# Scaling the values of four blocks in two halves, and one of these scalings at another place in GpSimd's queue

## The chip, the cores and the metric

The kernel runs on one core of one Trainium2 chip. The metric is the device time of one execution in microseconds (us), shorter is better; the time given for a kernel is the median of several runs. Before the change it was 153.32 us, median of 3 runs (153.32 to 153.71).

A core has five engines that run their own instruction queues in order and wait for each other through semaphores: TensorE (PE, matrix products; its weight loads are listed apart as PEld), VectorE (DVE), ScalarE (ACT), GpSimd (POOL) and SyncE (SP, which only issues transfers here). Transfers between device memory and the core's working memory are carried by 16 DMA engines, whichever queue issued them.

## What is computed

Two layers, one behind the other, on 4 sequences of 768 tokens. The first is a recurrence with 8 heads of width 64, each with its own decay; the second a feed-forward layer of the RWKV kind on its output.

```python
gamma = 1 - 2 ** (-5 - arange(H)); scale = 1 / sqrt(D)
for t in range(S):                                   # per batch b and head h
    state = gamma * state + outer(k[t], v[t])        # 64 x 64
    y[t] = scale * (q[t] @ state)
x = y with heads side by side                        # 4 x 768 x 512
xk = mu_k * x + (1 - mu_k) * x_prev                  # x_prev: one token before
xr = mu_r * x + (1 - mu_r) * x_prev
out = sigmoid(xr @ w_r) * (relu(xk @ w_k) ** 2 @ w_v)
```

Inputs and output are float32; matrix products take float16 operands.

## The kernel before

**Blocks.** The tokens are cut into 12 blocks of 256 (block n is tokens 256·(n mod 3) of sequence n div 3), and the recurrence is done block by block in its parallel form. For a block, with keys K, queries Q and values V: V is multiplied by a power of the head's decay, a different one for each token (`VS`, float16); K and Q are turned by PE; PE makes scores from them, DVE masks these (`A2`); PE makes the output from the masked scores and `VS`, and from Q and the state that the blocks before left; PE makes the block's share of the state from K and `VS`. Then comes the feed-forward layer of the block.

**Three kinds of blocks.** A block has 256 tokens and the memory 128 partitions, so two tokens lie in each partition, as i = 0 and 1. In blocks 0 and 1 these are neighbours (tokens 2p and 2p + 1). In blocks 2 to 5 (`WIDE`) and 6 to 11 (`HALF`) they are tokens p and p + 128: i = 0 is the first half of the block, i = 1 the second, and each half comes with a transfer of its own (256 KB of values each). In memory, `V32(n)` holds for each partition 8 heads x 128 numbers, i = 0 and 1 side by side within a head; `VS(n)` holds all of i = 0 ahead of all of i = 1. There are 4 buffers `V32` and 3 buffers `VS`, taken in turn.

**The order is written out by hand.** `ORDER` is a list of words, one for each step, such as `vs.3~p`: code `vs` (scale the values), block 3, engine p (p POOL, v DVE, a ACT, s SP); a number after @ names the banks of PE's result memory. The loop at the end of the kernel reads the words from the first to the last and emits each step's instructions, so that each engine's queue has its steps in the order of the list. Waits follow from what a step reads and writes. The steps that matter here:

- `lq`, `lk`, `lv`: load queries, keys, values of a block (function `load`); nearly all are issued by POOL. In a load of a block from 2 on, `lk` and `lv` are two transfers each. One transfer costs POOL an instruction (L230 or L235 in the profile).
- `vs`: scale the values (`scale_v`, L253). It is one instruction on DVE for ten of the blocks and on POOL for blocks 1 and 3.
- `C`: the block's share of the state, on PE (`state`; L384 for blocks 2 to 5). Blocks 2 and 5 are the last of their sequences; there the loop takes i = 0 alone. For blocks 3 and 4 it takes i = 0 and i = 1. `C` reads `VS`.
- `U`: the state carried on (`summed`; L419 on DVE, L241 for `U.3.0`, a copy on ACT). `G`: the state decayed (`decayed`, L424 on ACT).
- `S`, `M`: scores (L331) and their mask (L354, DVE). `I`, `Y`: output from the state (L441) and from the scores (L478), which reads `VS` too. `D`: output to the feed-forward layer's input (L514, DVE). `Tq`, `Tk`: queries and keys turned (L272, L278).
- `K`, `Qa`, `Qb`: product with w_k (L582 and L572), ReLU (L591), square (L603). `R`, `s`: product with w_r (L612), sigmoid (L618). `V`, `O`: product with w_v (L624), final product (L630). `wv`: load of w_v (L742).

The stretch of the list that the change touches, and what follows it up to the next loads:

```
lq.5~p Ek.3~a K.2.2@5 Qa.2.2~a K.2.3@4 M.4.1~v M.4.0~v Qa.2.3~a Qb.2.3~a lk.6~p S.3.1@67 M.3.1~v
S.3.0@01 vs.3~p C.3@23 U.3.0~a Qb.2.2~a K.2.1@4 Qa.2.1~a K.2.0@2 Qa.2.0~a I.3@45 lq.6~p vs.4~v
C.4@67 U.3.1~v X.2.1.1~v V.0.1.0@3 M.3.0~v V.1.0.0@2 G.3~a U.4.0~v I.4@01 X.2.1.3~v U.4.1~v J.3
Qb.1.3~a Y.4 Qb.2.0~a lk.5~p X.2.1.2~v ...
```

So POOL's queue is there: lq.5, lk.6 (two transfers), vs.3, lq.6, lk.5 (two), lk.7 (two), lv.5 (two). In the built program each load that POOL issues also waits, where its turn comes, for the landing of the load that POOL issued eight places before it: the loads take eight semaphores in turn. So lk.6's second transfer waits for the first half of lv.3, and what lk.6's first one waits for landed before that. C.3 writes banks 2 and 3, which S.4.0 had before, so that it waits for M.4.0 on DVE as well as for vs.3.

Of the kernel before, what the change touches and what calls it, by code (L numbers as in the profile page):

```python
# [30 lines left out]
X.0.0.1~v t.0.1.2~a X.0.0.2~v Tk.2@0 t.0.1.3~a t.0.0.0~a M.1.0~v X.0.0.0~v z.2@4 Y.1 t.0.1.1~a
X.0.0.3~v Ek.2~a K.0.0@0 K.0.1@6 lq.4~p U.1.1~v G.1~a wr~p lk.4~p D.1~v dx.1~v X.1.0.2~v X.1.0.0~v
K.0.2@1 Qa.0.0~a Qb.0.0~a Qa.0.2~a lq.3~p X.1.0.1~v X.1.0.3~v X.1.1.0~v Qa.0.1~a K.0.3@0 Qa.0.3~a
lk.3~p vs.2~v Tq.2@1 X.1.1.2~v K.1.3@6 K.1.0@0 C.2@7 U.2.0~v lv.3~p Eq.2~a S.2.1@23 M.2.1~v S.2.0@45
M.2.0~v Qb.0.3~a lv.4~p K.1.1@1 X.1.1.1~v Qa.1.0~a t.0.1.0~a K.1.2@7 I.2@23 Qb.0.1~a Qa.1.1~a wv.0~p
Qb.0.2~a Tq.4@01 Eq.4~a Y.2 Qa.1.3~a Qb.1.1~a X.0.1.3~v X.1.1.3~v R.1.1@4 Tk.4@01 Ek.4~a J.2 R.1.0@6
# [6 lines left out]
J.4 D.4~v dx.4~v R.2.0@6 Qb.2.1~a V.0.0.1 O.0.0~v X.3.0.1~v Eq.5~a Qb.1.2~a V.1.0.1 X.3.0.2~v
O.1.0~v Tq.6@01 Eq.6~a Tk.6@45 Ek.6~a st.0.0~s lk.7~p st.1.0~s V.1.1.0@3 V.1.1.1 O.1.1~v s.2.0~a
R.2.1@0 s.2.1~a lv.5~p X.3.0.0~v X.3.0.3~v Tk.7@67 Ek.7~a G.4~a S.6@45 M.6~v Tk.5@23 Ek.5~a vs.5~v
V.2.0.0@0 K.3.2@1 Qa.3.2~a K.3.0@6 S.5.0@23 M.5.0~v S.5.1@45 C.5@1 U.5.0~v K.3.3@7 Qb.3.2~a Qa.3.0~a
lq.7~p K.3.7@6 Qa.3.3~a Qa.3.7~a lv.6~p lq.8~p vs.6~v M.5.1~v V.2.0.1 st.0.1~s I.5@67 O.2.0~v
st.2.0~s C.6@23 U.6.0~a U.6.1~v U.6.2~v K.3.6@1 Qa.3.6~a lk.9~p X.3.1.3~v Y.5 Tq.7@45 Eq.7~a U.6.3~v
X.3.1.2~v I.6@01 J.5 X.3.1.0~v D.5~v X.3.1.1~v Qb.3.3~a G.6~a V.2.1.0@2 K.3.1@3 V.2.1.1 O.2.1~v
Qb.3.7~a Qa.3.1~a Qb.3.1~a dx.5~v K.3.4@4 K.3.5@5 Qa.3.5~a X.5.0.0~v X.5.0.3~v R.3.1@2 s.3.1~a  # L50
lv.7~p Qa.3.4~a X.5.0.1~v Qb.3.4~a R.3.0@5 R.4.0@2 s.3.0~a s.4.0~a Qb.3.0~a X.5.0.2~v vs.7~v K.5.2@4
S.7@67 st.1.1~s M.7~v Qb.3.5~a Y.6 Qb.3.6~a lv.10~p C.7@23 U.7.0~v X.5.1.1~v Qa.5.2~a K.5.0@5
R.4.1@6 Qa.5.0~a D.6~v s.4.1~a V.4.0.0@4 V.4.0.1 V.3.1.0@5 U.7.1~v Qb.5.0~a X.5.1.3~v U.7.2~v I.7@01
X.5.1.2~v U.7.3~v Tq.8@67 Eq.8~a X.5.1.0~v O.4.0~v lv.8~p vs.8~v Qb.5.2~a lq.10~p lk.8~p Tk.8@23
# [30 lines left out]
def kernel(  # L85
# [136 lines left out]
    def load(x, d, split, a=None):
        def go(e, n, j0=0, j1=NJ):
            b, t0 = n // NB, n % NB * TM
            hs = slice(2 * j0, 2 * j1)
            src = x[b, hs, t0 : t0 + TM, :]
            dst = staged(a)[:, hs] if (a, n, j0) in EARLY else d(n)[:, hs]
            if split and (half(n) or wide(n)):
                for i in range(2):
                    e.dma_start(  # L230
                        out=dst[:, :, i * D : i * D + D],
                        in_=src[:, i * P : i * P + P].rearrange("h p d -> p h d"),
                    )
            else:
                e.dma_start(out=dst, in_=src.rearrange("h (p i) d -> p h (i d)", i=2))  # L235

        return go
# [12 lines left out]
        return go  # L250

    def scale_v(e, n):
        e.tensor_tensor(  # L253
            out=VS(n), in0=V32(n).rearrange("p h (i d) -> p i h d", i=2),
            in1=gks[:, int(half(n) or wide(n)), :, :, None].to_broadcast([P, 2, H, D]), op=ALU.mult,
        )
# [543 lines left out]
```

## Time and profile before

| what | us |
|---|---|
| time, median of 3 runs | 153.32 (153.32 to 153.71) |
| time of the profiled execution | 153.28 |
| its span, first to last instruction | 151.4 |
| PE busy | 143.4 (95%) |
| DVE busy | 127.8 (84%) |
| ACT busy | 103.6 (68%) |
| POOL busy | 55.3 (37%), all of it in the first 76 us |

The granted clock of PE was 1.000 over the whole span. The profile consists of a page (busy time, the span in 40 slices, the chain of work that ended last, the costliest groups of instructions) and of views asked from the trace. A row of a timeline gives the start, the duration of a run of equal instructions from the start of its first to the end of its last, the engine, the line, the operation, what it writes and reads, the shape, the count, and in brackets how long the engine was idle before it and what ended this. Instructions on one engine may overlap slightly in such rows, since the next one starts before the last one's end.

### The profile page before, as it was taken

Reading aid. Unit: us, or ns where it says so; the run is one execution under the profiler, and the core shown is the slowest. Engines: PE = TensorE matmul, PEld = TensorE weight load, DVE = VectorE, ACT = ScalarE, POOL = GpSimd, SP = SyncE. Lnnn points to the kernel's source line nnn. Section 1 sums busy time; section 2 is a strip of 40 time slices with the busy share of each in tenths; the row PEclk is TensorE's granted clock in tenths of the full one; section 3 lists DMA queues with packets and bytes.
Section 4 is the critical chain, followed back from the end, with each engine's and each line's share of the span. In section 5 each row is a group of like instructions: output and inputs, shape, how many; then the busy total and the mean of one; then the engine's idle time right before and its main releaser. Section 6 shows DMA issues by size and latency. Waiting matters only on the chain.

```text
span 151.4 us, 5541 instructions
## 1 busy us (share of the span) xinstructions
PE 143.4 (95%) x2426; PEld 82.8 (55%) x2426; DVE 127.8 (84%) x212; ACT 103.6 (68%) x195; POOL 55.3 (37%) x65
## 2 busy tenths in 40 slices
PE   7878799999999999999999999999999999999991
PEld 3345487757754554547465564548456444655450
DVE  7886999999989999999999999999799999400432
ACT  3565979899844795779567786999604756839420
POOL 7953998577957309996710000000000000000000
PEclk9999999999999999999999999999999999999999
DMA  5999999999999999999999019301000005500433
GB/s 140 219 229 197 207 231 192 168 251 212 196 167 202 233 262 107 256 300 198 231 173 126 7 38 283 105 35 45 0 4 0 4 0 211 205 0 0 148 133 139
DMA packets 45624, 22.16 MB, mean 146 GB/s; under 512 B 37400, under 2 KB 41248, under 8 KB 45600
## 3 DMA queue, kind: packets, MB, share of 16 engines
q0 software_dynamic: 38704, 14.42, 74.5%
q1 hardware_dynamic: 6592, 7.21, 14.3%
q8 instruction: 19, 0.31, 0.8%
q10 hardware_dynamic: 304, 0.18, 0.4%
q14 instruction: 5, 0.04, 0.1%
HBM read 24.16 MB, written 6.29 MB: 201 GB/s over the span
## 4 chain that ended last, share of the span: by engine, by line
PE 73%; DMA 12%; POOL 11%; issue 1%; DVE 0%; POOLq 0%
PE ps L624 27%; PE ps L572 14%; DMA v<-in_v_dram 12%; PE ps L612 12%; PE ps L582 8%; PE ps L278 3%; POOL q L235 3%; POOL k L230 2%; PE ps L441 2%; POOL vs L253 2%; POOL v L230 2%; PE ps L366 1%; PE ps L462 1%; PE ps L642 1%; PE ps L318 1%
## 5 line engine op out<-in xcount | busy, mean ns | idle before, releaser
L624 PE MATMUL ps<-wv,k2s 128*128 128x512 f16 x184 | 44.1, 380 | 0.0
L591 ACT ACTIVATE kr<-ps 128x512 f32<-128x512 f32 x48 | 27.9, 594 | 12.5 <-PE ps L582 6.5
L624 PEld LDWEIGHTS <-k2s 128*128 128x128 f16 x184 | 17.1, 98 | 18.9 <-ACT k2s L603 0.4
L630 DVE SCALAR_TENSOR_TENSOR os<-ps,rs 128x512 f32<-128x512 f32 x23 | 15.6, 684 | 11.9 <-ACT rs L618 9.4
L612 PE MATMUL ps<-wr,xr 128*128 128x512 f16 x96 | 23.5, 379 | 0.0
L582 PE MATMUL ps<-xk,wk 128*128 128x256 f16 x192 | 23.2, 273 | 0.0
L572 PE MATMUL ps<-xk,wk 128*128 128x512 f16 x96 | 23.0, 379 | 0.0
L618 ACT ACTIVATE rs<-ps 128x512 f32<-128x512 f32 x24 | 13.6, 597 | 12.9 <-PE ps L612 12.1
L230 POOL DMA_DIRECT2D k<-in_k_dram x20 | 17.8, 903 | 10.3 <-PE ps L384 6.7
L582 PEld LDWEIGHTS <-wk 128*128 128x128 f16 x192 | 18.1, 98 | 3.7
L241 ACT COPY qT<-ps 128x1024 f16<-128x1024 f16 (+1 forms) x13 | 12.3, 946 | 9.5 <-PE ps L278 7.8
L558 DVE SCALAR_TENSOR_TENSOR xr<-dx,mu,xT 128x256 f16<-128x256 f32 (+1 forms) x32 | 17.9, 577 | 0.1
L230 POOL DMA_DIRECT2D v<-in_v_dram x18 | 16.0, 911 | 3.6 <-DMA wr<-in_moe_w_r_dram 1.9
L558 DVE SCALAR_TENSOR_TENSOR xk<-dx,mu,xT 128x256 f16<-128x256 f32 (+1 forms) x32 | 17.0, 579 | 0.2
L354 DVE TENSOR_TENSOR a<-ps,c_sb 128x1024 f16<-128x1024 f32 (+1 forms) x14 | 14.6, 1066 | 0.9 <-PE ps L339 0.6
L603 ACT ACTIVATE k2s<-kr 128x512 f16<-128x512 f32 x24 | 14.8, 631 | 0.3
L612 PEld LDWEIGHTS <-xr 128*128 128x128 f16 x96 | 9.0, 97 | 10.7 <-issue 0.5
L572 PEld LDWEIGHTS <-wk 128*128 128x128 f16 x96 | 9.1, 98 | 10.5
L599 ACT ACTIVATE k2s<-kr 128x512 f16<-128x512 f32 x24 | 14.5, 627 | 0.3
L241 ACT COPY kT<-ps 128x1024 f16<-128x1024 f16 (+1 forms) x13 | 12.2, 945 | 2.2 <-PE ps L272 1.7
L529 DVE TENSOR_TENSOR dx<-xT 128x1024 f32<-128x1024 f32 x11 | 13.4, 1221 | 0.2
L253 DVE TENSOR_TENSOR vs<-v,csm_sb 128x1024 f16<-128x1024 f32 x10 | 12.2, 1217 | 0.2 <-DMA v<-in_v_dram 0.2
(73 smaller groups left out, 165.6 us busy)
## 6 DMA issues: line engine op xcount, KB each, us to landing
out_dram<-os SPq DMA_DIRECT2D x23, 256.0 KB, 2.4
v<-in_v_dram POOLq DMA_DIRECT2D x18, 256.0 KB, 7.7
q<-in_q_dram POOLq DMA_DIRECT2D x11, 256.0 KB, 8.4
k<-in_k_dram POOLq DMA_DIRECT2D x21, 128.0 KB, 8.8
v<-in_v_dram POOLq DMA_DIRECT2D x2, 512.0 KB, 7.2
wk<-in_moe_w_k_dram POOLq DMA_DIRECT2D x2, 512.0 KB, 10.4
wv<-in_moe_w_v_dram POOLq DMA_DIRECT2D x2, 512.0 KB, 10.4
wr<-in_moe_w_r_dram POOLq DMA_DIRECT2D x1, 512.0 KB, 8.7
```

The costliest lines, as they stand in the source:

```text
L230: e.dma_start(out=dst[:, :, i * D : i * D + D], in_=src[:, i * P : i * P + P].rearrange("h p d -> p h d"),)
L241: e.copy(out=out, in_=in_)
L253: e.tensor_tensor(out=VS(n), in0=V32(n).rearrange("p h (i d) -> p i h d", i=2), in1=gks[:, int(half(n) or wide(n)), :, :, None].to_broadca ...
L354: nc.vector.tensor_tensor(out=a_full(n)[:, i, :, j0:j1], in0=pairs(banks("S", n, i, j0))[:, :, j0:j1], in1=(below if wide(n) else causal[: ...
L558: nc.vector.scalar_tensor_tensor(out=XM[w](k)[:, j, t0:t1], in0=DX(k)[:, j, t0:t1], scalar=mu[:, w * NCO + j : w * NCO + j + 1], in1=x[:, ...
L572: nc.tensor.matmul(banks("K", n, g), lhsT=wk16[:, co, g * P : g * P + P], rhs=XM[0](k)[:, co, :], start=(co == 0), stop=(co == NCO - 1),)
L582: nc.tensor.matmul(pz[:, i, :], lhsT=wk16[:, co, fo * P : fo * P + P], rhs=XM[0](k)[:, co, m * TM + t0 : m * TM + t1], start=(i == 0 and c ...
L591: nc.scalar.activation(out=kr, in_=banks("K", n, g, *u), func=AF.Relu)
L603: nc.scalar.activation(out=K2(n)[:, w * g : w * g + w, t0:t1], in_=kr.rearrange("p a t -> p (a t)").rearrange("p (i t) -> p i t", i=w), fu ...
L612: nc.tensor.matmul(banks("R", n, tb), lhsT=XM[1](k)[:, co, t : t + P], rhs=wr16[:, co, :], start=(co == 0), stop=(co == NCO - 1),)
L624: nc.tensor.matmul(banks("V", n, tb), lhsT=K2(n)[:, fo, tb * P : tb * P + P], rhs=wv16[:, fo, :], start=(fo == 0), stop=(fo == NFO - 1),)
L630: nc.vector.scalar_tensor_tensor(out=OS(2 * n + tb), in0=banks("V", n, tb), scalar=1.0 / (KSC * KSC), in1=RS(2 * n + tb), op0=ALU.mult, op ...
```

## The change

1. For blocks 2 to 5 the buffer of values is used as two halves, one behind the other: `part_v(n, i)` is the i-th half of `V32(n)`, 8 heads x 64 numbers without gaps. The two transfers of `lv` write one half each. The transfers read what they read before.
2. For these blocks `scale_v` is two instructions of 128 x 512 in place of one of 128 x 1024, each for one half, and each waits for its own half's transfer. That is so on DVE for blocks 2, 4 and 5, and on POOL for block 3.
3. In `ORDER`, `vs.3~p` stands ahead of `lk.6~p`, no longer behind `S.3.0`. Of the engines' queues only POOL's is changed by this: lq.5, vs.3 (two instructions), lk.6 (two transfers), lq.6 and so on as before.

The words of `ORDER` are wrapped anew, so that the full diff replaces the whole list; apart from the one word that is moved it is the same. What is left of it:

```diff
-lq.5~p Ek.3~a K.2.2@5 Qa.2.2~a K.2.3@4 M.4.1~v M.4.0~v Qa.2.3~a Qb.2.3~a lk.6~p S.3.1@67 M.3.1~v
-S.3.0@01 vs.3~p C.3@23 U.3.0~a Qb.2.2~a K.2.1@4 Qa.2.1~a
+lq.5~p Ek.3~a K.2.2@5 Qa.2.2~a K.2.3@4 M.4.1~v M.4.0~v Qa.2.3~a Qb.2.3~a vs.3~p lk.6~p S.3.1@67 M.3.1~v
+S.3.0@01 C.3@23 U.3.0~a Qb.2.2~a K.2.1@4 Qa.2.1~a
...
+    def part_v(n, i):
+        f = V32(n).rearrange("p h x -> p (h x)")
+        return f[:, i * H * D : i * H * D + H * D].rearrange("p (h d) -> p h d", h=H)
+
...
                 for i in range(2):
                     e.dma_start(
-                        out=dst[:, :, i * D : i * D + D],
+                        out=part_v(n, i) if d is V32 and wide(n) else dst[:, :, i * D : i * D + D],
                         in_=src[:, i * P : i * P + P].rearrange("h p d -> p h d"),
                     )
...
     def scale_v(e, n):
+        if wide(n):
+            for i in range(2):
+                e.tensor_tensor(
+                    out=VS(n)[:, i], in0=part_v(n, i),
+                    in1=gks[:, 1, i, :, None].to_broadcast([P, H, D]), op=ALU.mult,
+                )
+            return
         e.tensor_tensor(
             out=VS(n), in0=V32(n).rearrange("p h (i d) -> p i h d", i=2),
             in1=gks[:, int(half(n) or wide(n)), :, :, None].to_broadcast([P, 2, H, D]), op=ALU.mult,
         )
```

In the built program each of the two instructions for block 3 also waits for a product on PE of block 0 that read the same buffer `VS` before (the order of the loads gave that wait until now). For blocks 2 and 5, `C` waits for the first half's instruction alone; for blocks 3 and 4 its products wait for each half's instruction as they come to it.

More of the change, by code (lines that the diff above doesn't have):

```diff
@@ L31 @@
[L31 to L36, printed above, removed]
@@ L43 @@
[L43 to L48, printed above, removed]
@@ L49 @@
[L49 to L54, printed above, removed]
@@ new lines @@
+Eq.1~a vs.1~p lq.2~p Tk.1@7 Ek.1~a M.0.0.0.2~v M.0.1.2.4~v Y.0 D.0~v t.0.0.3~a t.0.0.2~a t.0.0.1~a
+lv.2~p z.2@4 S.1.1@23 M.1.1~v C.1@01 U.1.0~v z.2@4 I.1@23 S.1.0@67 X.0.0.1~v t.0.1.2~a X.0.0.2~v Tk.2@0
+t.0.1.3~a t.0.0.0~a M.1.0~v X.0.0.0~v z.2@4 Y.1 t.0.1.1~a X.0.0.3~v Ek.2~a K.0.0@0 K.0.1@6 lq.4~p
+U.1.1~v G.1~a wr~p lk.4~p D.1~v dx.1~v X.1.0.2~v X.1.0.0~v K.0.2@1 Qa.0.0~a Qb.0.0~a Qa.0.2~a lq.3~p
+X.1.0.1~v X.1.0.3~v X.1.1.0~v Qa.0.1~a K.0.3@0 Qa.0.3~a lk.3~p vs.2~v Tq.2@1 X.1.1.2~v K.1.3@6 K.1.0@0
@@ new lines @@
+C.2@7 U.2.0~v lv.3~p Eq.2~a S.2.1@23 M.2.1~v S.2.0@45 M.2.0~v Qb.0.3~a lv.4~p K.1.1@1 X.1.1.1~v Qa.1.0~a
+t.0.1.0~a K.1.2@7 I.2@23 Qb.0.1~a Qa.1.1~a wv.0~p Qb.0.2~a Tq.4@01 Eq.4~a Y.2 Qa.1.3~a Qb.1.1~a
+X.0.1.3~v X.1.1.3~v R.1.1@4 Tk.4@01 Ek.4~a J.2 R.1.0@6 Qa.1.2~a s.1.0~a X.0.1.2~v X.0.1.1~v X.0.1.0~v
+R.0.1@5 s.0.1~a s.1.1~a R.0.0@7 s.0.0~a S.4.1@01 Qb.1.0~a D.2~v dx.2~v X.2.0.2~v X.2.0.0~v S.4.0@23
+Tq.3@4 Eq.3~a X.2.0.1~v wv.1~p X.2.0.3~v Tk.3@7 lq.5~p Ek.3~a K.2.2@5 Qa.2.2~a K.2.3@4 M.4.1~v M.4.0~v
@@ new lines @@
+O.1.1~v s.2.0~a R.2.1@0 s.2.1~a lv.5~p X.3.0.0~v X.3.0.3~v Tk.7@67 Ek.7~a G.4~a S.6@45 M.6~v Tk.5@23
+Ek.5~a vs.5~v V.2.0.0@0 K.3.2@1 Qa.3.2~a K.3.0@6 S.5.0@23 M.5.0~v S.5.1@45 C.5@1 U.5.0~v K.3.3@7
+Qb.3.2~a Qa.3.0~a lq.7~p K.3.7@6 Qa.3.3~a Qa.3.7~a lv.6~p lq.8~p vs.6~v M.5.1~v V.2.0.1 st.0.1~s I.5@67
+O.2.0~v st.2.0~s C.6@23 U.6.0~a U.6.1~v U.6.2~v K.3.6@1 Qa.3.6~a lk.9~p X.3.1.3~v Y.5 Tq.7@45 Eq.7~a
+U.6.3~v X.3.1.2~v I.6@01 J.5 X.3.1.0~v D.5~v X.3.1.1~v Qb.3.3~a G.6~a V.2.1.0@2 K.3.1@3 V.2.1.1 O.2.1~v
@@ new lines @@
+C.8@67 O.3.1~v st.2.1~s st.3.1~s Y.7 dx.6~v D.7~v Tq.10@23 V.3.0.1 Eq.10~a G.7~a dx.7~v X.6.0.2~v
+V.4.1.0@5 R.5.1@2 s.5.1~a K.5.3@0 Qa.5.3~a R.5.0@2 U.8.0~v O.3.0~v V.4.1.1 lv.9~p lk.10~p lq.9~p
+Tk.10@01 s.5.0~a U.8.1~v X.6.0.1~v Ek.10~a X.6.0.0~v Tk.9@23 Ek.9~a K.5.1@7 Qa.5.1~a X.6.0.3~v K.6.0@4
+lq.11~p Qb.5.1~a Qa.6.0~a U.8.2~v I.8@01 vs.9~v S.8@23 M.8~v O.4.1~v st.4.1~s K.6.4@7 Qa.6.4~a vs.10~v
+X.6.1.2~v K.6.2@6 C.9@23 Qa.6.2~a Qb.6.2~a U.9.0~a Y.8 U.9.1~v D.8~v U.9.2~v U.9.3~v X.6.1.3~v Qb.5.3~a
@@ new lines @@
+Tq.9@45 V.5.1.0@6 V.5.1.1 O.5.1~v Eq.9~a lk.11~p K.6.3@7 Qa.6.3~a K.6.7@4 Qa.6.7~a V.5.0.0@7 C.10@45
+Qb.6.0~a X.6.1.0~v S.9@23 M.9~v G.9~a Qb.6.3~a Tq.11@01 Eq.11~a V.5.0.1 dx.8~v X.6.1.1~v st.4.0~s
+K.6.1@6 Qb.6.7~a Qa.6.1~a Qb.6.1~a X.8.0.3~v X.8.0.0~v U.10.0~v U.10.1~v K.6.5@2 Qa.6.5~a st.3.0~s
+lv.11~s K.6.6@0 Qa.6.6~a Qb.6.6~a R.6.0@6 s.6.0~a O.5.0~v U.10.2~v U.10.3~v R.7.0@2 s.7.0~a R.6.1@7
+s.6.1~a I.9@45 X.8.0.2~v S.10@23 Tk.11@01 Ek.11~a X.8.0.1~v K.8.1@7 Qb.6.5~a Qa.8.1~a Qb.8.1~a vs.11~v
@@ new lines @@
+st.5.1~s K.8.0@6 C.11@01 M.10~v Qb.6.4~a X.8.1.0~v X.8.1.2~v Y.9 D.9~v G.10~a U.11.0~v st.5.0~s U.11.1~v
+U.11.2~v Qa.8.0~a I.10@23 V.6.1.0@7 V.6.1.1 O.6.1~v V.6.0.0@4 V.6.0.1 I.11@01 S.11@67 M.11~v dx.9~v
+V.7.1.0@5 V.7.1.1 Y.10 D.10~v dx.10~v X.9.0.3~v X.9.0.0~v Y.11 Qb.8.0~a X.9.0.2~v R.7.1@6 s.7.1~a
+X.9.0.1~v V.7.0.0@7 V.7.0.1 K.8.3@6 O.7.0~v X.9.1.0~v D.11~v X.8.1.1~v Qa.8.3~a Qb.8.3~a K.8.2@2
+Qa.8.2~a Qb.8.2~a X.8.1.3~v dx.11~v X.11.1.0~v X.11.1.1~v X.9.1.1~v V.8.1.0@6 K.9.2@3 X.11.0.0~v K.9.6@7
@@ new lines @@
+Qa.9.6~a V.8.1.1 Qa.9.2~a Qb.9.2~a X.11.0.3~v K.9.5@7 K.9.3@3 K.9.0@2 Qa.9.0~a Qb.9.6~a V.8.0.0@0
+V.8.0.1 Qb.9.0~a Qa.9.5~a Qb.9.5~a Qa.9.3~a O.7.1~v st.7.1~s X.9.1.2~v X.11.0.1~v O.6.0~v K.9.7@1
+R.8.1@7 s.8.1~a K.9.1@5 R.8.0@7 X.9.1.3~v X.11.0.2~v st.6.1~s O.8.1~v R.9.1@4 R.9.0@6 K.11.0@3 K.11.3@2
+s.8.0~a Qa.9.1~a Qb.9.1~a Qb.9.3~a V.10.0.0@5 V.9.0.0@7 Qa.11.0~a Qb.11.0~a Qa.11.3~a s.9.0~a K.9.4@6
+R.10.0@2 Qa.9.7~a X.11.1.3~v st.6.0~s K.11.1@1 Qa.11.1~a Qa.9.4~a K.11.2@3 Qb.9.7~a Qb.9.4~a Qa.11.2~a
@@ L81 @@
+X.11.1.2~v O.8.0~v st.7.0~s st.8.1~s st.8.0~s V.9.1.0@1 V.10.1.0@6 s.10.0~a V.9.1.1 V.10.0.1 s.9.1~a
+O.9.1~v st.9.1~s Qb.11.2~a Qb.11.3~a O.10.0~v st.10.0~s R.10.1@4 V.9.0.1 s.10.1~a O.9.0~v R.11.1@4
+V.10.1.1 Qb.11.1~a V.11.0.0@7 R.11.0@5 s.11.0~a st.9.0~s Vc.11.1.1@1 s.11.1~a O.10.1~v st.10.1~s
+Oc.11.1.1~v V.11.0.1 O.11.0~v st.11.0~s sc.11.1.1~a Vc.11.1.0@4 Oc.11.1.0~v sc.11.1.0~s
 """
```

51 lines of the change are left out of this document (14 added, 37 removed).

## The prediction

> **What bounds the kernel now.** I read the page first, then the chain of waits, then PE's waits from 38 us on, then the timelines of the engines around the change.
>
> ```profile
> span 151.4 us, 5541 instructions
> ```
>
> ```profile
> 25.54 10.37 DMA v<-in_v_dram
> ...
> 35.98 1.91 POOL vs L253
> ...
> 37.93 0.44 PE ps L384 x16
> ...
> 148.28 0.42 DVE os L649
> ```
>
> Followed back from 148 us, the chain that ended last stays on PE until 37.93: the second half of block 3's values lands at 25.54 + 10.37 = 35.91, POOL scales the whole block from 35.98 to 37.89, and at 37.93 PE begins C.3 (L384). From there to 148 us it is PE alone. PE's waits from 38 us on (its row at 37.93 still belongs to that view) say the same; there is one:
>
> ```profile
> PE ps L384 <- POOL vs L253: 0.3, 1, 0.3
> ```
>
> So the time can only fall by what PE idles at this place, and all that is gained must then be carried through 110 us in which PE has no gap. How close the other engines stand shows in the busy times of the next stretch (PE, PEld, DVE, ACT, POOL):
>
> ```profile
> 38.50:56.00 17.50, 17.50 (x334) 9.57 (x334) 17.00 (x24) 12.04 (x24) 9.10 (x11) 1.00 1.71 211
> ```
>
> PE is busy for 17.50 of 17.50 us and DVE for 17.00. DVE is the engine that could hold PE back once PE is earlier.
>
> **What PE could gain at C.3.** PE's timeline at the wait, and at another place with the same two kinds of products and no wait:
>
> ```profile
> 36.98 0.62 PE L331 MATMUL ps<-qT,kT 64*128 64x128 f16 x16
> 37.93 0.44 PE L384 MATMUL ps<-vs,k 128*64 128x64 f16 x16 [0.33 <-POOL vs L253]
> 38.30 1.92 PE L582 MATMUL ps<-xk,wk 128*128 128x256 f16 x16
> ...
> 40.38 0.44 PE L384 MATMUL ps<-vs,k 128*64 128x64 f16 x16
> 40.76 1.90 PE L624 MATMUL ps<-wv,k2s 128*128 128x512 f16 x8
> 42.59 0.42 PE L441 MATMUL ps<-qT,tg 64*64 64x128 f16 x12
> ...
> 55.94 0.62 PE L331 MATMUL ps<-qT,kT 64*128 64x128 f16 x16
> 56.49 0.32 PE L384 MATMUL ps<-vs,k 128*64 128x64 f16 x8
> ```
>
> At 56.49 the products of L384 start 0.55 us after the start of the scores before them; at 37.93 it is 0.95. Without the wait C.3 would start at 36.98 + 0.55 = 37.53. But C.3 also waits for the mask M.4.0, the second of the three here:
>
> ```profile
> 35.17 3.54 DVE L354 TENSOR_TENSOR a<-ps,c_sb 128x1024 f16<-128x1024 f32 x3
> 38.63 1.22 DVE L253 TENSOR_TENSOR vs<-v,csm_sb 128x1024 f16<-128x1024 f32 x1
> 39.76 0.42 DVE L419 TENSOR_TENSOR t<-ps,tg 128x256 f32<-128x256 f32 x1
> ...
> 40.49 1.22 DVE L354 TENSOR_TENSOR a<-ps,c_sb 128x1024 f16<-128x1024 f32 x1
> 41.90 0.42 DVE L419 TENSOR_TENSOR tg<-ps,tg 128x256 f16<-128x256 f32 x1 [0.20 <-ACT tg L424]
> ```
>
> One of three starts (3.54 − 1.22)/2 = 1.16 after the one before, so the second ends at 35.17 + 1.16 + 1.22 = 37.55. With 0.04 for the signal, as between POOL's end at 35.98 + 1.91 = 37.89 and 37.93, C.3 starts at 37.56 to 37.59. The gain here is at most 37.93 − 37.56 = **0.37 us**.
>
> **POOL: does block 3's scaling come in time?** POOL's timeline:
>
> ```profile
> 30.09 0.77 POOL L742 DMA_DIRECT2D wv<-in_moe_w_v_dram  x1
> 31.23 0.75 POOL L742 DMA_DIRECT2D wv<-in_moe_w_v_dram  x1 [0.37 <-DMA q<-in_q_dram]
> 32.33 0.89 POOL L235 DMA_DIRECT2D q<-in_q_dram  x1 [0.35 <-issue]
> 33.31 0.88 POOL L230 DMA_DIRECT2D k<-in_k_dram  x1
> 34.58 0.87 POOL L230 DMA_DIRECT2D k<-in_k_dram  x1 [0.39 <-issue]
> 35.98 1.90 POOL L253 TENSOR_TENSOR vs<-v,csm_sb 128x1024 f16<-128x1024 f32 x1 [0.53 <-DMA v<-in_v_dram]
> 37.83 0.94 POOL L235 DMA_DIRECT2D q<-in_q_dram  x1
> 38.76 2.64 POOL L230 DMA_DIRECT2D k<-in_k_dram  x3
> 42.85 0.88 POOL L230 DMA_DIRECT2D k<-in_k_dram  x1 [1.45 <-DMA wv<-in_moe_w_v_dram]
> ```
>
> The keys' second transfer, at 34.58, waits for the first half of block 3's values, so that half is there by 34.58 at the latest; lq.5 ends at 33.22. The first instruction starts between these two. The second starts when the second half lands, at 35.98. What a half costs on POOL no row shows. If time goes with size it is 1.90/2 = 0.95; if all of it is fixed, 1.90. I take 0.95: DVE's rows above go nearly with size (128x256 in 0.42, 128x1024 in 1.22, so 1.04 ns an element and 0.15 us fixed), and POOL's 1.90 us hold more work per element, not less. Then the first half ends by 35.53 and the second at 36.93, 0.6 us ahead of 37.56. With 1.90 each it would be 34.58 + 3.80 = 38.38.
>
> Moving vs.3 ahead of lk.6 puts two transfers behind it: they go out at 36.93 and 37.8 in place of 33.31 and 34.58, then lq.6 at 38.7 (before 37.83), lk.5's two and lk.7's first, 0.87 us later each. The next one, at 42.85, is held by a landing of w_v for 1.45 us, and the delay ends there: lk.7's first would end at about 42.3. Who needs these loads? Landing times, of block 3's and 4's values, of w_v, and PE's first use of block 6's keys:
>
> ```profile
> DMA to landing us min/median/max: 8.1/8.9/10.4
> ```
>
> ```profile
> DMA to landing us min/median/max: 9.7/10.4/11.1
> ```
>
> ```profile
> 49.24 0.44 PE L278 MATMUL ps<-c_sb,k 64*64 64x64 f16 x32
> ```
>
> At 8.9 us the keys' second half lands at 37.8 + 8.9 = 46.7, 2.2 us ahead of PE's 49.24 − 0.37. Even at 11.1 it is only 48.9. And the DMA engines have work meanwhile: w_v's second half, issued at 31.23, lands some 11 us later, past 42. I take nothing for the move; without that cover lk.6 would be 3.6 us late.
>
> **DVE: two instructions in place of one, three times.**
>
> ```profile
> 24.27 1.22 DVE L253 TENSOR_TENSOR vs<-v,csm_sb 128x1024 f16<-128x1024 f32 x1
> 25.97 0.42 DVE L419 TENSOR_TENSOR tg<-ps,tg 128x256 f16<-128x256 f32 x1
> ...
> 51.38 1.28 DVE L630 SCALAR_TENSOR_TENSOR os<-ps,rs 128x512 f32<-128x512 f32 x2
> ```
>
> Two of 128 x 512 behind each other take 1.28 us from first start to last end, one of 128 x 1024 takes 1.22: **+0.06 to 0.07 us** per block. Bounds: nothing below, and 0.25 above (two starts 0.69 apart, the length of one such instruction, against 1.13 from the vs at 38.63 to what follows it).
>
> The Trainium skill, page "VectorE: DVE Perf Modes", section "The DRAIN you can't avoid", speaks against this part of the change: the next instruction cannot issue until the one before has left the pipeline, so it says to minimize the count. By that rule the two would take 2 × 0.69 = 1.38 us, 0.16 more than one, and I.4 below would start 0.10 later and the time come out at 153.05, not 152.95. The rows here show the next instruction starting some 0.08 us before the one ahead ends (39.76 against 38.63 + 1.22), so I keep them.
>
> Block 2, at 24.27: behind the next instruction U.2 starts at 25.97, when C.2 on PE has ended; it could have started at about 25.81, so 0.07 is absorbed. C.2 needs the first half only, a gain of a few hundredths at most. Block 5 the same: C.5 at 56.49 needs the first half, and the mask behind waits for PE's scores. Block 4, at 38.63, counts.
>
> **Carried through.** With PE 0.37 earlier and DVE 0.07 later from 38.63 on:
>
> - K.2.0, the second eight of the L582 row (38.30 + 0.96 = 39.26, now 38.89), needs the copy U.3.0 on ACT. ACT is at a square until 38.40, so this copy hardly moves:
>
> ```profile
> 37.77 0.63 ACT L603 ACTIVATE k2s<-kr 128x512 f16<-128x512 f32 x1
> 38.38 0.37 ACT L241 CAST tg<-ps 128x256 f16<-128x256 f32 x1
> ...
> 40.32 0.60 ACT L591 ACTIVATE kr<-ps 128x512 f32<-128x512 f32 x1 [0.28 <-PE ps L582]
> 40.82 1.05 ACT L424 ACTIVATE tg<-t,csm_sb 128x64 f16<-128x64 f32 x4
> ```
>
>   it would end at about 38.7, 0.15 ahead.
> - C.4 now wants 40.38 − 0.37 = 40.01; vs.4 ends at 38.63 + 1.22 + 0.07 = 39.92: 0.05 to spare behind the 0.04 for the signal.
> - I.4 wants 42.59 − 0.37 = 42.22. It needs U.4.0, which waited 0.20 us for G.3 on ACT. G.3 sits behind a ReLU that waits for PE, so it moves by 0.37 to 40.45 and ends at 41.50. DVE comes to U.4.0 at 41.90 − 0.20 + 0.07 = 41.77 and ends it at 42.19: just in time, to a few hundredths.
>
> Behind that DVE and ACT start again on PE's results, so all moves together. Sum, against the profiled execution's own 153.28 (span 151.4 and 1.88 around it): −0.37 for C.3, 0 for the move, 0 for DVE: span 151.0, time 152.91. That execution is 0.04 below the median of 153.32, so I forecast **152.95 us**, 0.24% faster. What a measurement of this kernel can tell from no change is about 0.3%, 0.46 us; the forecast lies inside that.
>
> **Rivals.**
>
> 1. *DVE becomes the bound.* If a pair of halves costs the upper 0.25 us, vs.4 ends at 40.10, C.4 starts at 40.14 (0.13 lost), and U.4.0 ends at 42.37, so that I.4 starts 0.19 behind 42.22: gain 0.37 − 0.19 = 0.18, time 153.14. If M.4.0 too is late by that much, block 2's delay not being absorbed, C.3 slips to 37.7 as well and the gain is near nothing: 153.1 to 153.35. For it: DVE's 17.00 of 17.50. Against it: the 1.28 us row.
> 2. *POOL's cost is per instruction: slower.* At 1.90 for a half, vs.3 ends at 38.38, not at 37.89: C.3 is 0.49 later than now, 153.8. It turns from gain to loss where a half costs over (37.89 − 34.58)/2 = 1.65 us. Against it: the fixed share on DVE is 0.15 of 1.22.
> 3. *The loads into gapless halves land later: slower.* w_v's first half, issued at 30.09, lands 9.7 us later, at 39.8, and PE uses it at 40.76, now 40.39. Six half-blocks of values (blocks 2 to 4) land ahead of it in the same queue. If each took over 0.1 us more, the gain begins to go; over 0.16, the time is above today's; at 0.3 it is 1.8 − 0.94 = 0.9 us above: 154.2. Against it: the values of block 1 go into memory without gaps already, all 512 KB in one transfer, and the chain has it from issue to landing in 8.07 us, where halves of 256 KB took 8.1 to 10.4.
>
> ```profile
> 5.52 8.07 DMA v<-in_v_dram
> ```
>
> 4. *The change does nothing.* C.3 is held by something the profile does not name: 153.3. Against it: the chain names vs.3 to 0.04 us.
>
> **From these to the numbers.** Forecast as worked out (152.8 to 153.1): 0.60. Rival 1: 0.15; rival 2: 0.06; rival 3: 0.10; rival 4: 0.04; 0.05 for a gain above 0.46 by something the rows do not show. The range reaches down to 152.65 (0.37, hundredths at C.2, and the spread of the runs) and up to 153.75, just short of rival 2's end. Faster by over 0.3%: 0.05 and the quarter of the forecast's own share in which the spread carries it over the line, together 0.22. Slower by over 0.3%: rivals 2 and 3 and a little of rival 1, 0.17. The rest, 0.61, is within it.
>
> **What would show each step.** Right: C.3 (L384 at about 37.6) with no idle time behind POOL; POOL's two instructions of about 0.95 us, the second starting at 36.0; the w_v wait on POOL still near 42.8; two DVE instructions of about 0.69 us, 0.60 apart; no new wait of PE behind 38 us. Wrong: a wait of C.4, V or I.4 for DVE (rival 1), POOL's halves above 1.5 us (rival 2), landings of values above 10.4 us or PE waiting for w_v (rival 3).

## The result, and the profile after

| kernel | time, us | ratio to before (95% interval) |
|---|---|---|
| before, runs of the same comparison | 153.30, median of 22 (152.95 to 157.01) | |
| after | 154.06, median of 22 (153.45 to 155.04) | 1.0059 (1.0042 to 1.0077) |

The change makes the kernel 0.6% slower. The forecast was 152.95 us and the range ended at 153.75: both missed, on the wrong side. Medians here and below are of all runs; the ratios leave out those that lie over 1.5% above the fastest of their kernel, which are one run of before here and one in each of two later comparisons, two of the twelve of `e1_halves_late` and eight of the twelve of `e4_extra_read`. The profiled execution of the changed kernel took 154.69 us. Most of the kernel's line numbers are 8 higher now (L582 is L590, L384 is L392); the halves are scaled at L256.

The chain that ended last, by engine, from the page of before:

```profile
PE 73%; DMA 12%; POOL 11%; issue 1%; DVE 0%; POOLq 0%
```

and of after:

```profile
span 152.9 us, 5547 instructions
...
PE 83%; DVE 8%; DMA 4%; ACT 2%; issue 1%; DVEq 0%; POOLq 0%
```

POOL has left the chain, as it was meant to, and DVE has come into it. PE's timeline of before and after at block 2's K.2.2 (the sixteen products of xk), S.3.0 and C.3; first the kernel before:

```profile
25.54 0.32 PE L384 MATMUL ps<-vs,k 128*64 128x64 f16 x8
...
35.12 1.92 PE L582 MATMUL ps<-xk,wk 128*128 128x256 f16 x16
```

and after:

```profile
25.79 0.32 PE L392 MATMUL ps<-vs,k 128*64 128x64 f16 x8
...
35.60 0.27 PE L590 MATMUL ps<-xk,wk 128*128 128x256 f16 x1 [0.17 <-DVE xk L566]
...
36.78 1.98 PE L590 MATMUL ps<-xk,wk 128*128 128x256 f16 x15 [0.91 <-DVE xk L566]
38.69 0.62 PE L339 MATMUL ps<-qT,kT 64*128 64x128 f16 x16
39.45 0.44 PE L392 MATMUL ps<-vs,k 128*64 128x64 f16 x16
```

From C.2 to C.3 it was 37.93 − 25.54 = 12.39 us and is 39.45 − 25.79 = 13.66, so 1.27 more. (The 0.25 by which C.2 itself is late arose before 10 us, and the runs differ there in either direction; so this distance, from C.2 to C.3, is what the runs below are compared by.) The loss is there ahead of C.3: K.2.2 waits for DVE's xk, which before it did not. The chain that ended last shows by which way the delay reaches C.3 at 39.45: it goes from two xk over two masks, both on DVE.

```profile
35.47 1.65 DVE xk L566 x2
37.13 2.27 DVE a L362 x2
```

DVE's timeline of the kernel before at the four xk of K.2.2:

```profile
33.58 1.67 DVE L558 SCALAR_TENSOR_TENSOR xk<-dx,mu,xT 128x256 f16<-128x256 f32 x4
```

and DVE's and POOL's after, each instruction by itself:

```profile
33.82 0.48 DVE L566 SCALAR_TENSOR_TENSOR xk<-dx,mu,xT 128x256 f16<-128x256 f32 x1
34.23 1.32 DVE L566 SCALAR_TENSOR_TENSOR xk<-dx,mu,xT 128x256 f16<-128x256 f32 x1
35.47 1.26 DVE L566 SCALAR_TENSOR_TENSOR xk<-dx,mu,xT 128x256 f16<-128x256 f32 x1
36.65 0.47 DVE L566 SCALAR_TENSOR_TENSOR xk<-dx,mu,xT 128x256 f16<-128x256 f32 x1
...
34.23 1.04 POOL L256 TENSOR_TENSOR vs<-v,csm_sb 128x512 f16<-128x512 f32 x1 [0.78 <-PE ps L339]
35.35 1.10 POOL L256 TENSOR_TENSOR vs<-v,csm_sb 128x512 f16<-128x512 f32 x1
36.40 1.81 POOL L231 DMA_DIRECT2D k<-in_k_dram  x2
...
43.48 0.88 POOL L231 DMA_DIRECT2D k<-in_k_dram  x1 [1.77 <-DMA wv<-in_moe_w_v_dram]
```

The first and the fourth xk take what one took before, 0.48 to within 0.01. The second and the third take 1.32 and 1.26, and they are the two during which POOL scales a half: POOL's first half ends at 34.23 + 1.04 = 35.27, the second xk at 35.55; POOL's second half ends at 36.45, the third xk at 36.73. Each ends 0.28 us behind POOL. So DVE did not get on while POOL's product ran: 0.84 + 0.78 = 1.62 us. An xk has two operands in the working memory (dx and xT), and so have POOL's products. The masks M, beside which POOL's scaling ran before, have one operand in PE's result memory, and in the kernel before they were not slowed (three in 3.54 us from 35.17 to 38.71, with POOL's scaling at 35.98 to 37.88).

That is the theory, A: *POOL's scaling of block 3, moved into the time of DVE's xk of block 2, keeps DVE out.* Its rivals: B, *the halves, the gapless buffer or DVE's pairs cost the time, not the place*; C, *the move costs because lk.6 and the loads behind it go out late*.

### The profile page after: what moved, and what is told of

Its sections match the earlier page's. It is cut to its first block, busy times and chain, and to the rows that moved or that the text cites. A ratio compares the mean times of both kernels' runs of the same rounds, so it can differ in the third digit from the quotient of the medians.

```text
span 152.9 us, 5547 instructions
## 1 busy us (share of the span) xinstructions
PE 143.7 (94%) x2426; PEld 82.9 (54%) x2426; DVE 129.5 (85%) x215; ACT 103.6 (68%) x195; POOL 55.5 (36%) x66
## 4 chain that ended last, share of the span: by engine, by line
PE 83%; DVE 8%; DMA 4%; ACT 2%; issue 1%; DVEq 0%; POOLq 0%
PE ps L632 27%; PE ps L620 14%; PE ps L580 14%; PE ps L590 12%; DVE a L362 5%; DMA v<-in_v_dram 4%; PE ps L286 3%; PE ps L449 2%; PE ps L280 2%; PE ps L486 1%; PE ps L374 1%; PE ps L470 1%; PE ps L650 1%; PE ps L326 1%; PE ps L339 1%
## 5 line engine op out<-in xcount | busy, mean ns | idle before, releaser
L590 PE MATMUL ps<-xk,wk 128*128 128x256 f16 x192 | 23.5, 273 | 1.1 <-DVE xk L566 1.1
L620 PE MATMUL ps<-wr,xr 128*128 128x512 f16 x96 | 23.5, 379 | 0.0
L590 PEld LDWEIGHTS <-wk 128*128 128x128 f16 x192 | 18.2, 98 | 5.1 <-issue 1.3
L566 DVE SCALAR_TENSOR_TENSOR xk<-dx,mu,xT 128x256 f16<-128x256 f32 (+1 forms) x32 | 18.6, 630 | 0.2
L236 POOL DMA_DIRECT2D q<-in_q_dram x12 | 10.8, 901 | 0.5 <-issue 0.3
```

The lines of the kernel that those rows point to most:

```text
L566: nc.vector.scalar_tensor_tensor(out=XM[w](k)[:, j, t0:t1], in0=DX(k)[:, j, t0:t1], scalar=mu[:, w * NCO + j : w * NCO + j + 1], in1=x[:, ...
L590: nc.tensor.matmul(pz[:, i, :], lhsT=wk16[:, co, fo * P : fo * P + P], rhs=XM[0](k)[:, co, m * TM + t0 : m * TM + t1], start=(i == 0 and c ...
L620: nc.tensor.matmul(banks("R", n, tb), lhsT=XM[1](k)[:, co, t : t + P], rhs=wr16[:, co, :], start=(co == 0), stop=(co == NCO - 1),)
```

## The experiments

Times are medians of twelve runs, but of four for `f2_read_behind_issue`, two for `g2_issue_then_read` and `f3_after_again`, and eight for `f4_after_third`. Distances are from the start of C.2 to the start of C.3 (in `e1_halves_late` to those of its products that waited); before it is 12.39 us, after 13.66.

| run | what | distance | time, us | ratio (95% interval) |
|---|---|---|---|---|
| `e1_halves_late` | after, vs.3 back at its old place | 12.72 | 153.35 | 1.0008 (0.9996 to 1.0019) |
| `e2_whole_early` | before, vs.3 moved only | 12.02 | 153.31 | 1.0003 (0.9991 to 1.0016) |
| `e3_store_only` | after, block 3's scaling stores and reads nothing | 12.02 | 152.89 | 0.9979 (0.9963 to 0.9995) |
| `e4_extra_read` | before, one more product on POOL | 15.62 | 157.56, see below | 1.0025 (1.0007 to 1.0043) |
| `f1_gated` | after, vs.3 starts behind the last xk | 12.02 | 152.96 | 0.9990 (0.9974 to 1.0006) |
| `f2_read_behind_issue` | before, one more product, behind lk.6 | 13.25 | 154.37 | 1.0079 (1.0052 to 1.0106) |
| `f3_after_again` | after | 13.60 | 154.67 (154.79 profiled) | 1.0100 (1.0062 to 1.0138) |
| `f4_after_third` | after | 12.81 | 153.66 (153.55 profiled) | 1.0042 (1.0014 to 1.0070) |
| `g1_gated_again` | as `f1_gated` | 12.02 | 153.23 | 0.9986 (0.9960 to 1.0011) |
| `g2_issue_then_read` | before, a product behind lq.5's issue | 17.64 | 159.11 | 1.0359 (1.0286 to 1.0433) |

**The place undone, the halves kept (`e1_halves_late`).**

```diff
-Qa.2.3~a Qb.2.3~a vs.3~p lk.6~p S.3.1@67 M.3.1~v S.3.0@01 C.3@23
+Qa.2.3~a Qb.2.3~a lk.6~p S.3.1@67 M.3.1~v S.3.0@01 vs.3~p C.3@23
```

> The change as a whole, but block 3's scaling stays where it was before the change, behind both transfers of lk.6 (the halves, their buffer and all else kept). Theory A (POOL's scaling now runs at 34.2 to 36.5 us beside DVE's products xk of block 2, which read two operands from SBUF, and holds two of the four back by 0.8 us each): the scaling begins at about 35.45, when the products have ended, and runs beside the masks; all four products take about 0.48 us, C.3 starts near 37.65, time about 153.05, 0.998 of before. Rival B (the halves, the gapless buffer or DVE's pairs cost the time, not the place of the scaling): the time stays near 153.9 to 154.1, 1.005 of before.

The loss is gone: 153.35, so it isn't in the halves, the buffer or the pairs. DVE's, POOL's and PE's timelines:

```profile
33.64 1.67 DVE L566 SCALAR_TENSOR_TENSOR xk<-dx,mu,xT 128x256 f16<-128x256 f32 x4
35.23 2.35 DVE L362 TENSOR_TENSOR a<-ps,c_sb 128x1024 f16<-128x1024 f32 x2
...
36.23 2.05 POOL L256 TENSOR_TENSOR vs<-v,csm_sb 128x512 f16<-128x512 f32 x2
...
38.33 0.41 PE L392 MATMUL ps<-vs,k 128*64 128x64 f16 x14 [0.47 <-POOL vs L256]
```

All xk are as before, and the two masks beside POOL's halves are not slowed either. The 0.3 us that A expected as a gain didn't come: in this run POOL was through with lk.6 only at 36.2, since one of its loads at 23.5 us had waited 0.79 us for the landing of another, and two halves take 2.05 us where the whole took 1.90. Behind two issues, the halves were worth nothing in this run.

**The move alone, as a whole block (`e2_whole_early`).**

```diff
-Qa.2.3~a Qb.2.3~a lk.6~p S.3.1@67 M.3.1~v S.3.0@01 vs.3~p C.3@23
+Qa.2.3~a Qb.2.3~a vs.3~p lk.6~p S.3.1@67 M.3.1~v S.3.0@01 C.3@23
```

> The kernel before, with only block 3's scaling moved ahead of lk.6: one instruction over the whole block, old buffer, so that it waits for the second half at about 36.0 us. Theory A: by then the four products xk have ended (35.25), nothing is held; C.3 stays at 37.9, time 153.3 within 0.2, ratio 1.000. Rival C (the move itself costs: lk.6 and the loads behind it go out late and are missed): slower, 153.9 to 154.1, with a wait of PE, ACT or DVE for a load behind 40 us.

POOL's timeline, and PE's only wait behind 38 us:

```profile
35.19 1.90 POOL L253 TENSOR_TENSOR vs<-v,csm_sb 128x1024 f16<-128x1024 f32 x1 [1.68 <-DMA v<-in_v_dram]
37.04 1.82 POOL L230 DMA_DIRECT2D k<-in_k_dram  x2
...
58.62 1.02 PE L624 MATMUL ps<-wv,k2s 128*128 128x512 f16 x4 [0.33 <-issue]
```

lk.6 goes out at 37.04, even later than in the changed kernel, and nothing waits for a load behind 40 us: this speaks against rival C, and `f1_gated` below, with the loads as late and no wait at all, leaves nothing of it. The second half landed by 35.19, not at 36.0 as expected, so that C.3 did not wait for POOL. Yet the time is not better: PE lost 0.33 us at 58.3 to something that the profile does not name. No other run here shows it, with the same loads late; what it was stays open.

**Stores in place of block 3's scaling (`e3_store_only`).**

```diff
             for i in range(2):
+                if n == 3:
+                    e.memset(VS(n)[:, i], 0.0)
+                    continue
                 e.tensor_tensor(
```

> The change as a whole, but POOL's two instructions for block 3 store zeros and read no values: the scaling of block 3's values is left out, the two instructions stand at the same place of POOL's order. They need no load, so they may run earlier than the scaling did. Theory A (what holds DVE is that both read SBUF): all four xk of block 2 at about 0.48 us, C.3 bound by the mask on DVE near 37.56, time about 152.95, ratio 0.998. Rival B (halves, layout, DVE pairs): near 153.9 to 154.1. Rival C (late loads): as here lk.6 goes out as early as before, 153.0 too; e2 tells it from A.

```profile
33.42 1.01 POOL L257 MEMSET vs<- 128x512 f16 x2
...
33.88 1.67 DVE L569 SCALAR_TENSOR_TENSOR xk<-dx,mu,xT 128x256 f16<-128x256 f32 x4
```

POOL writes the same buffer beside the first two xk and holds none of them: four in 1.67. So writing alone does not keep DVE out; what the stores lack is the product's reading, and its arithmetic, which no run here takes apart from it. The time, 152.89, is 0.43 below before, but in this kernel block 3's values are not scaled and lk.6 goes out 2 us earlier than in the changed one; what the change brings without the hold is read from `f1_gated`.

**A hold put into the kernel before (`e4_extra_read`).**

```diff
-lq.5~p Ek.3~a
+lq.5~p xt.0~p Ek.3~a
...
+        e.tensor_tensor(
+            out=OS(3).rearrange("p (a t) -> p a t", a=4), in0=zero[:, None, :].to_broadcast([P, 4, P]),
+            in1=zero[:, None, :].to_broadcast([P, 4, P]), op=ALU.mult,
+        )
```

> The kernel before, with one more product on POOL, 128x512 of two SBUF operands into a buffer that is free at that time, behind lq.5 (it starts at about 33.3 us and takes about 1.0 us; lk.6 goes out 1.0 us later). Theory A: it overlaps the first xk of block 2 (33.58 to 34.05 before), which is held until it ends: one xk near 1.2 us in place of 0.48; K.2 waits for it and the time rises by 0.3 to 0.7, about 153.75, ratio 1.003. Rivals B and C (no hold between POOL and DVE): xk all at 0.48, time 153.3, ratio 1.000.

Four of the twelve runs lie at 153.50 to 153.91, as A expected; the other eight, the profiled one among them, lie at 156.5 to 159.0. DVE's and POOL's timelines of that one:

```profile
34.02 1.24 DVE L558 SCALAR_TENSOR_TENSOR xk<-dx,mu,xT 128x256 f16<-128x256 f32 x1
35.19 0.87 DVE L558 SCALAR_TENSOR_TENSOR xk<-dx,mu,xT 128x256 f16<-128x256 f32 x2
35.98 2.97 DVE L558 SCALAR_TENSOR_TENSOR xk<-dx,mu,xT 128x256 f16<-128x256 f32 x1
...
33.92 1.05 POOL L748 TENSOR_TENSOR os<-zero 128x512 f32<-128x512 f32 x1
34.90 1.82 POOL L230 DMA_DIRECT2D k<-in_k_dram  x2
36.73 1.92 POOL L253 TENSOR_TENSOR vs<-v,csm_sb 128x1024 f16<-128x1024 f32 x1
```

The first xk is held by the additional product to 35.26, as expected; this product reads a tile of zeros, so that the hold is not tied to the buffer of the values. The fourth starts 0.75 us ahead of POOL's scaling of block 3, while a transfer is still being issued, and is held all the same, to 38.95. This was the start of theory D: POOL keeps DVE out from when its product stands behind a running issue.

**D, two ways (`f2_read_behind_issue`, `g2_issue_then_read`).** Both are the kernel before with the same additional product: in the first behind lk.6, in the second behind lq.5, with two stores of zeros ahead of lq.5 that shift it into the time of the xk.

```diff
-Qb.2.3~a lk.6~p S.3.1@67
+Qb.2.3~a lk.6~p xt.0~p S.3.1@67
```

> The kernel before, with the additional POOL product of two SBUF operands (128x512) behind both transfers of lk.6, so that it stands queued while the second of them is being issued (34.6 to 35.45) and starts at 35.45, when the last xk has ended (35.25). Theory A as it stands (POOL holds DVE from its own start on): all four xk at 0.48 us; block 3's scaling ends 0.5 to 0.6 later (36.5 to 38.4), C.3 at 38.45, time 153.8, ratio 1.003. Theory D, from the fourth xk of the run with the additional read ahead of lk.6, which started 0.75 us before POOL's scaling and was held to its end (2967 ns): POOL keeps DVE out already while the issue ahead of its product runs; the fourth xk is held from 34.8 to about 36.8, PE waits over 1 us for K.2, time 154.5 or more.

```profile
33.78 1.67 DVE L558 SCALAR_TENSOR_TENSOR xk<-dx,mu,xT 128x256 f16<-128x256 f32 x4
...
35.16 0.87 POOL L230 DMA_DIRECT2D k<-in_k_dram  x1 [0.32 <-issue]
36.05 1.05 POOL L748 TENSOR_TENSOR os<-zero 128x512 f32<-128x512 f32 x1
```

Inconclusive for D: the second issue began at 35.16, when the last xk (which began 0.48 ahead of the end of this row, 34.97) was already running, so that no xk fell into it. POOL was 0.6 us later than expected, and so was C.3.

```diff
-lq.5~p Ek.3~a
+xt.1~p lq.5~p xt.0~p Ek.3~a
```

> The kernel before with two stores of zeros on POOL ahead of lq.5 (about 0.9 us together, they read nothing) and the additional product of two SBUF operands (128x512) right behind lq.5's issue, so that some xk of block 2 starts while that issue runs and the product stands behind it. Theory A (DVE is held from POOL's own start on): the xk that start during the issue take 0.48 us; the first that starts behind the product's start is held to 0.28 us past its end. Theory D (held already while the issue ahead of the product runs): the first xk that starts more than 0.1 us into the issue is held to 0.28 us past the product's end, 1.5 to 2.3 us long; PE waits over 1 us for it.

```profile
34.21 1.91 DVE L558 SCALAR_TENSOR_TENSOR xk<-dx,mu,xT 128x256 f16<-128x256 f32 x1
36.05 3.76 DVE L558 SCALAR_TENSOR_TENSOR xk<-dx,mu,xT 128x256 f16<-128x256 f32 x1
...
33.88 0.89 POOL L235 DMA_DIRECT2D q<-in_q_dram  x1
34.78 1.05 POOL L749 TENSOR_TENSOR os<-zero 128x512 f32<-128x512 f32 x1
35.77 1.82 POOL L230 DMA_DIRECT2D k<-in_k_dram  x2
37.60 1.92 POOL L253 TENSOR_TENSOR vs<-v,csm_sb 128x1024 f16<-128x1024 f32 x1
```

D came true twice. The first xk starts 0.33 us into lq.5's issue and is held from there to 36.12, 0.29 behind the end of the product that follows (35.83). The second starts 0.28 us into lk.6's first issue and is held through both issues and the scaling, to 39.81. POOL's issues by themselves hold nothing: with a load next that still had to wait (`f2_read_behind_issue`, lk.6's first at 33.97, two xk started beside it), xk stayed at 0.48.

**The changed kernel twice more (`f3_after_again`, `f4_after_third`).** Its 22 runs lie in two groups, 12 at 153.45 to 154.10 and 10 at 154.49 to 155.04.

> The changed kernel once more, to see why its runs lie in two groups (about 153.9 and 154.7). Theory A: the time goes with the number of xk that POOL's two halves hold and by how much, which depends on when the two halves land (34.2 and 35.35 in the first profile, two held by 0.84 and 0.78, 154.69). A profiled run near 153.9 shows one of them held, or both for a shorter time, 0.7 us less in all; one near 154.7 shows 1.6 us in all again. Rival: the holds are the same in all runs and the difference arises elsewhere.

> The same again, for a second point: the sum of what the four xk take above 4 x 0.48 us should differ between runs by what their times differ by; with the rival it does not.

The first of these profiled runs took 154.79 and shows two held xk, of 1.27 and 1.26. The second took 153.55; DVE's and POOL's timelines:

```profile
33.41 1.28 DVE L566 SCALAR_TENSOR_TENSOR xk<-dx,mu,xT 128x256 f16<-128x256 f32 x3
34.60 1.27 DVE L566 SCALAR_TENSOR_TENSOR xk<-dx,mu,xT 128x256 f16<-128x256 f32 x1
...
34.28 1.31 POOL L256 TENSOR_TENSOR vs<-v,csm_sb 128x512 f16<-128x512 f32 x1 [0.87 <-DMA v<-in_v_dram]
35.55 1.21 POOL L256 TENSOR_TENSOR vs<-v,csm_sb 128x512 f16<-128x512 f32 x1
```

Here DVE reached the xk 0.4 us earlier, at 33.41, while the first half landed no earlier. Three xk had started before POOL's first half did; only the fourth was held, by 0.79, and the masks stood beside POOL's second half. POOL waits for DVE in its turn: its first half starts during the third xk and takes 1.31. One hold gives a distance 0.42 above before's, two give 1.21 and 1.27. So the two groups are, as far as three profiled runs show it, one and two holds.

**The repair (`f1_gated`, `g1_gated_again`).** A copy of one column of the last xk on POOL, ahead of vs.3, lets POOL wait for DVE.

```diff
-Qb.2.3~a vs.3~p lk.6~p
+Qb.2.3~a gv~p vs.3~p lk.6~p
...
+    def gate_v(e):
+        k, m = place[2]
+        e.tensor_copy(out=OS(3)[:, 0:1], in_=XM[0](k)[:, 3, 0:1])
```

> The change as a whole, with one small instruction on POOL ahead of block 3's scaling: a copy of one column of the last xk of block 2 into a free buffer, so that the scaling cannot start before DVE's four products have ended. Theory A (POOL's reads beside xk are the whole loss): all four xk at 0.48 us; the copy at about 35.3 takes 0.1 to 0.2, the scaling runs 35.5 to 37.6 beside the masks, which are not slowed (1.22); C.3 near 37.65, time 153.0, ratio 0.998. If the loads that go out behind the scaling cost (rival C), or the halves (rival B): 153.5 or more, with a wait behind C.3.

> The version with the small copy ahead of block 3's scaling once more, for its ratio to the kernel before: from its first profile (C.3 0.39 us earlier against the positions ahead of it) 153.0 and a ratio of 0.998; from its first timing 0.999.

```profile
33.72 1.67 DVE L566 SCALAR_TENSOR_TENSOR xk<-dx,mu,xT 128x256 f16<-128x256 f32 x4
...
35.46 0.18 POOL L754 CAST os<-xk 128x1 f32<-128x1 f16 x1 [1.90 <-DVE xk L566]
35.60 2.04 POOL L256 TENSOR_TENSOR vs<-v,csm_sb 128x512 f16<-128x512 f32 x2
...
37.71 0.44 PE L392 MATMUL ps<-vs,k 128*64 128x64 f16 x16
```

The halves and the early place are all there, the loads are as late as in the changed kernel (lk.6 at 37.59), the four xk take 1.67 together, and C.3 starts without a wait, 12.02 us behind C.2 (37.71 − 25.69): 0.37 better than before, to the hundredth the same as with stores. The times are 152.96 and 153.23 against 153.21 and 153.38 for the kernel before in the same comparisons. Both are below it and clearly below the changed kernel; against before the intervals of both include 1, so a gain of 0.1% is likely and not shown.

## Why the prediction was wrong

**The step that failed.** In the part on POOL the two halves were laid from 34.58 to 36.93 and the step ended with "I take nothing for the move; without that cover lk.6 would be 3.6 us late". What the move does to POOL's own queue was followed to the last load. What stands *beside* POOL at its new time was not looked at: the row of four xk at 33.58 to 35.25 is not among those that the prediction shows or weighs. None of its rivals has this mechanism. Rival 1 has C.3 slip with a late M.4.0, which is what came, but by dearer pairs on DVE, which did not come. The moved work stopped running beside masks and ran beside xk, and cost DVE 0.8 us for each xk that it met, one or two of them. The masks stand behind the xk in DVE's queue, and C.3 waits for the second of them, M.4.0, which ends at 37.13 + 2.27 = 39.40 in the changed kernel. So the holds reach C.3 in full: added to the 12.02 us that stand without one, two of 1.62 together make 13.64 (measured 13.66), the two of `f3_after_again`, 1.57, make 13.59 (13.60), and the one of `f4_after_third`, 0.79, makes 12.81 (12.81). Against before's 12.39 that is 1.27, 1.21 and 0.42 lost. K.2.2's wait alone would have cost less: S.3.0 behind it starts at 38.69, and with the 0.55 of the prediction C.3 could have followed at 39.24.

No row of before showed the hold, since there POOL's two scalings ran beside instructions of DVE with an operand in PE's result memory, and this is where a written rule was needed. The Trainium skill, page "SBUF — State Buffer", section "Who interferes with whom", has it: a VectorE instruction with two SBUF inputs contends with a GpSimd instruction that reads SBUF, not with one that only writes it, and whichever issues first shuts the other out for its whole length. The traces agree: 0.48 against 1.32 and 1.26 us beside a product, 0.48 beside a store, and POOL's half at 1.31 in place of 1.03 when an xk was ahead of it. On who comes first they go beyond it: in `g2_issue_then_read` an xk that started ahead of POOL's product was held all the same. With the rows of before and the prediction's own times this mechanism makes a loss: the fourth xk, due at 35.25 − 0.48 = 34.77, meets POOL's first half, which ends at 35.53, and behind it ends at 36.01, 0.76 late. M.4.0 moves with it, to 37.55 + 0.76, and C.3 to 38.35, which is 0.42 later than 37.93: 153.70 us. The run with one hold lost 0.42. That the two agree to the hundredth is luck: in the runs a held xk ended 0.28 us behind POOL and not a whole 0.48, and with 0.28 the same sum gives C.3 at 38.15 and 153.50 us.

**The steps that held.**

- *C.3 could start 0.37 us earlier, with M.4.0 as the next bound.* Right: 12.39 − 12.02 = 0.37 in the runs without a hold in which POOL was in time; in the changed kernel itself C.3 no longer waits for POOL.
- *0.95 us for a half on POOL.* Nearly: 1.03 undisturbed (two in 2.04), so two cost 0.14 more than the whole. Rival 2's 1.90 is out.
- *The late loads harm nothing.* Right: the w_v wait stands at 43.48, and behind 40 us PE waits for nothing.
- *A pair on DVE costs 0.06 to 0.07 more.* Right; DVE's timeline of after at block 4 (block 2's pair takes the same):

```profile
40.45 1.28 DVE L256 TENSOR_TENSOR vs<-v,csm_sb 128x512 f16<-128x512 f32 x2
```

- *What is gained or lost at C.3 is carried to the end.* Right: from C.3 to the last group of PE's products it is 147.21 − 37.93 = 109.28 in before (start of that group 147.21), 109.26 in after (148.71) and 109.32 in the gated version (147.03).
- *Rival 3, halves that land later*: the first half landed by 34.2, where it was forecast by 34.58, no half loaded from 20 to 40 us took over 9.5 us to land (before 10.4), and PE waits nowhere for w_v. Not seen.

With the hold away, C.3 starts the forecast 0.37 us earlier, and the times, 152.96 and 153.23, lie within the range. The gain in time against before, 0.25 and 0.15, is less than 0.37 and is not shown.

## What to carry to other kernels

When work is moved on one engine, look at what every other engine does in the new time slot, not only at the queue that it was moved in, above all where POOL and DVE both read their operands from the working memory. Ask of each DVE instruction there whether its inputs come from PE's result memory or both from the working memory: POOL's products belong beside the former. Where a transfer's landing decides the moment, a small dependency that makes POOL wait for DVE's last such instruction costs 0.18 us and saves 0.8 to 1.6.

## What the runs showed of the hardware

POOL's hold can begin before POOL's product does. In `g2_issue_then_read`, with two issues and a product behind them, an xk that started 0.28 us into the first issue was held for 3.76 us, through both issues and the scaling; the product itself, 1.92 us, starts 1.55 us later in the trace. Why the first issue of the same two in `e4_extra_read`, at 34.90, let two xk through, and the second did not, was not tried; that lk.6's second transfer still waited for a landing then is a guess.

PE pays twice for a long idle stretch. In `g2_issue_then_read` PE stood idle for 4.04 us up to 39.86:

```profile
39.86 3.48 PE L582 MATMUL ps<-xk,wk 128*128 128x256 f16 x16 [4.04 <-DVE xk L558]
```

Its rows by the microsecond from 39 us on (the columns are the stretch, its length, busy time and count of PE, PEld, DVE, ACT and POOL, the granted clock, the DMA share and GB/s):

```profile
39.00:40.00 1.00, 0.14 (x1) 0.10 (x1) 1.00 (x2) 0.00 (x0) 1.00 (x2) 0.76 1.27 201
40.00:41.00 1.00, 0.98 (x5) 0.53 (x4) 1.00 (x3) 0.00 (x0) 1.00 (x2) 0.50 1.50 192
41.00:42.00 1.00, 1.00 (x7) 0.67 (x6) 1.00 (x2) 0.00 (x0) 1.00 (x2) 0.50 1.84 178
42.00:43.00 1.00, 1.00 (x7) 0.69 (x6) 0.87 (x1) 0.60 (x1) 0.14 (x1) 0.53 2.22 163
43.00:44.00 1.00, 1.00 (x29) 0.69 (x29) 0.21 (x1) 0.56 (x1) 0.00 (x0) 1.00 2.17 165
```

The granted clock is half for over 3 us after the pause, and K.2.2 takes 3.48 us in place of 1.92. The profiled run of `e4_extra_read` shows the same after 2.5 us idle (0.50 from 41 to 43 us); there the clock was still 1.00 from 39 to 40 us, when PE had started again. Its eight longer runs lie some 3 to 5 us above the other four, which fits the second hold and this together, but only one of the eight and none of the four was profiled. The mean granted clock is 0.978 to 0.989 in seven of the eight; the eighth, of 156.47, has 1.000. Two runs of `e1_halves_late`, of 156.97 and 157.05, have 0.989 too; neither was profiled, so whether a hold stands behind them is open. The 0.9 us that PE idles in the changed kernel left the clock at 1.000. The Trainium skill, page "TensorE: Matmul & The Clock Gate", section "HAM oscillation — how this bites in real kernels", says to avoid idle gaps of PE above some 3.4 us; here 2.5 was already enough.
